# Dealing the gate and up weights' contraction rows four neighbours to a partition

## The chip, the cores and the metric

One core of one Trainium2 chip runs the kernel. The metric is the device time of one execution in microseconds, as the median of several runs. Beside it there is one profiled execution, whose trace gives every duration below.

## The reference

The input is x, 2048 tokens of 512 features in bfloat16 (`A_x`). The tokens are normalized, and two branches work on the result; the input `B_x` is not used.

```python
def reference(A_x, A_w_r, A_w_i, B_x, B_w_gate, B_w_up, B_w_down):
    ...
    x = A_x
    xn = _layernorm(x, axis=-1)
    return x + _A_ref(xn, A_w_r, A_w_i) + _B_ref(xn, B_w_gate, B_w_up, B_w_down)
```

Branch A is a two-dimensional real Fourier transform over tokens and features, a product with complex weights (2048 x 257), and the inverse transform. Branch B is a gated feed-forward layer: gelu(xn Wg) times (xn Wu), then a product with Wd. Wg and Wu are 512 x 1792, Wd is 1792 x 512.

## The kernel before

**Tokens.** Partition p holds tokens 16p to 16p+15, so `x_t` and `xn` are [128, 16 chunks, 512 features]. A chunk c is the 128 tokens 16p+c. Normalization takes mean and variance of a chunk on DVE (`f_stats` line 339, `f_mean` line 342). Chunks 0 to 3 are then normalized on DVE (`f_norm_v`, line 345): chunk 0 in two halves of 256 features (`xn_`, line 386), the others whole. Chunks 4 to 15 are normalized on ACT with a scale and a bias for each token (line 456).

**Transposed tokens.** The feed-forward products contract over features, so they need tokens with features on the partitions: `xnT[b]`, [128, 4 blocks e, 4 chunks, 128 tokens]. Chunks 0 to 3 are transposed by PE, one block of 128 features at a time (`f_T`, line 351, xn as the stationary operand), and copied out of PSUM by DVE or ACT (`f_Tc`, line 354). Chunks 4 to 15 are transposed by DMA (line 459).

**Gate and up weights.** `Wg_sb` and `Wu_sb` are [128, 4, 1792]. Before the change partition i holds the rows i, 128+i, 256+i and 384+i (lines 222 and 223). They are loaded in column slices of 512, 512 and 768, between the loads of x, all on SP's queue (lines 281 to 306); the second slice of Wg comes in two halves of two blocks each. Block e of the weights meets block e of `xnT`, and four matmuls over e give one product of 128 outputs (`mm`, line 494; `mm_part`, line 502).

**Feed-forward units.** A unit is a range of tokens by a range of outputs. PE computes its gate product in PSUM (tag G, two buffers) and its up product (tag U, two buffers); ACT takes gelu (`f_ge`, line 507); DVE multiplies (`f_h`, line 512) into `hT`. The first units are small (one or two chunks), the later ones 512 tokens by 128 outputs. The products with Wd come last (`mm` in `down`, line 829), followed by the last spectral product (line 833), the sum with x (line 836) and the store.

**Spectral branch.** `forward` takes four chunks at a time (groups 0 to 3). The transform over features uses the symmetry of cosines and sines: `fold_a` (line 571) adds and subtracts features d and 511-d into `A`, `fold_b` (line 577) does the same with 256 features and gives `xf`, four kinds q of 128 features each. PE multiplies xf with `RF_t` (bp, line 589), ACT stores the result as `Bs` (line 559), and `group` multiplies that with the matrices F0 to F3 (dp, line 647), whose rows are the 128 folded features. The rest of the branch doesn't see the order of features.

**Order of the work.** The order of instructions on every engine is fixed when the program is built. Each step is added to a `Plan` with an assumed duration, a latency, a key, a release time and the buffers that it takes and gives back; `Plan.order` (line 149) plays them through and writes each engine's instructions in the order in which that play starts them. Its landing times for loads are the constants LAND, WG_LAND and WU_LAND (lines 308 to 311). At run time only semaphores hold an engine up, and each engine works through its list in order.

```python
    WG_LAND = [6.1] * 4 + [10.15] * 4 + [13.2] * 6
    WU_LAND = [7.6] * 4 + [11.7] * 4 + [15.2] * 6
...
        u = split("u_ps", "U", Wu_sb, (1001.4, 1001.5, 1003.1, 1003.5)[k] if k < 4 else 1000.5 + k, WU_LAND, (2, m, 1)[k] if k < 3 else m)
```

At the start PE runs 37 matmuls on zeros, transposes chunk 0, runs 11 more matmuls whose result isn't used (`spin_on`, line 324), and then begins with the gate product of chunk 0.

Of the kernel before, what the change touches and what calls it, by code (L numbers as in the profile page):

```python
# [10 lines left out]
P = 128  # L11
# [17 lines left out]
def _tables():  # L29

    cols, parts, off = {}, [], 0

    def add(name, arr):
        nonlocal off
        arr = np.asarray(arr, dtype=np.float64).reshape(P, -1)
        cols[name] = (off, arr.shape[1])
        parts.append(arr)
        off += arr.shape[1]

    p = np.arange(P)[:, None]
    G, a = np.arange(64) // 4, np.arange(64) % 4
    freq = 16 * a + 8 * (G % 2) + G // 2
    ka = freq[None, :]
    RF = np.zeros((P, NC, 2, 64))
    for c in range(NC):
        th = 2 * np.pi * ((16 * p + c) * ka % S) / S
        RF[:, c, 0] = np.cos(th)  # L50
        RF[:, c, 1] = -np.sin(th)
        RF[:, c, 1, 0] = np.where(p[:, 0] % 2 == 0, 1.0, -1.0)

    d = np.arange(P)[:, None] + 0.5
    j = np.arange(P)[None, :]
    j1 = np.where(j == 0, 128, j)
    FB = [np.cos(2 * np.pi * 2 * j * d / D), np.sin(2 * np.pi * 2 * j1 * d / D),  # L60
          np.cos(2 * np.pi * (2 * j + 1) * d / D), np.sin(2 * np.pi * (2 * j + 1) * d / D)]
    for q in range(4):
        add(f"F{q}", FB[q])

    c = np.arange(NC)[:, None]
    kb = np.arange(NC)[None, :]
    cosk = np.cos(2 * np.pi * c * kb / NC)  # L70
    sink = np.sin(2 * np.pi * c * kb / NC)
    ph = 2 * np.pi * c * (64 + 128 * (kb - 8)) / S
    lo = kb < 8
    alt = np.where(np.arange(P) % 2 == 0, 1.0, -1.0)

    def packed(m0, m, back):
        out = np.zeros((NC, 2, 4, 2, NC, 4))
        for r in range(2):
            for r2 in range(2):
                for a in range(4):  # L80
                    out[:, r, a, r2, :, a] = (m0 if a == 0 else m)[r][r2]
        out = out.reshape(P, P)
        return out.T if back else out

    gen = [[cosk, -sink], [sink, cosk]]
    z_ri = np.where(lo, -sink, 0.0)
    z_ri[:, 0] = np.where(np.arange(NC) % 2 == 0, 1.0, -1.0)
    z = [[np.where(lo, cosk, 0.0), z_ri],
         [np.where(lo, 0.0, np.cos(ph)), np.where(lo, 0.0, -np.sin(ph))]]
    add("L", packed(gen, gen, False))  # L90
    add("L0", packed(z, gen, False))
    for q in range(4):
        add(f"I{q}", FB[q].T)
    add("M", packed(gen, gen, True))
    add("M0", packed(z, gen, True))

    RI = np.zeros((2, 64, NC, P))
    kac = freq[:, None]
    pr = np.arange(P)[None, :]
    sc = 2.0 / (S * D)  # L100
    for cc in range(NC):
        th = 2 * np.pi * ((16 * pr + cc) * kac % S) / S
        RI[0, :, cc] = sc * np.cos(th)
        RI[1, :, cc] = -sc * np.sin(th)
        RI[1, 0, cc] = sc * alt
    def low(a):
        return a.reshape(P, -1).astype(np.float32).astype(ml_dtypes.bfloat16)

    h, kb, a = np.arange(P) // 64, np.arange(P) // 4 % 16, np.arange(P) % 4
    base = 16 * a + 8 * h + 128 * kb
    ks = np.where((h == 0) & (a == 0) & (kb >= 8), 64 + 128 * (kb - 8), base)
    idx = np.zeros((P, 3), dtype=np.int32)
    idx[:, 0] = ks
    idx[:, 1] = (S - ks) % S
    idx[0, 1] = S // 2
    idx[:, 2] = (S - base - 8) // 8
    return low(np.concatenate(parts, axis=1)), cols, low(RF), low(RI), idx
# [82 lines left out]
def kernel(  # L202
# [16 lines left out]

    x_v = A_x.rearrange("b (p c) d -> p c (b d)", c=NC)  # L220
    out_v = out.rearrange("b (p c) d -> p c (b d)", c=NC)
    wg_v = B_w_gate.rearrange("(e i) f -> i e f", e=NE)
    wu_v = B_w_up.rearrange("(e i) f -> i e f", e=NE)
    wd_v = B_w_down.rearrange("(fc f) d -> f fc d", fc=NFC)

    pc = ctx.enter_context(tc.tile_pool(name="pc", bufs=1))
# [121 lines left out]
    def f_T(c, e0, n):  # L348
        tiles["T", c, e0] = tp = ps.tile([P, n, P], BF16, name="tp", tag="S", bufs=4)
        for e in range(n):  # L350
            T_.transpose(tp[:, e], xn[:, c, (e0 + e) * P:(e0 + e + 1) * P], ident)  # L351

    def f_Tc(c, e0, n, copy=V.tensor_copy):
        copy(out=xnT[0][:, e0:e0 + n, c, :], in_=tiles["T", c, e0][:])  # L354
# [19 lines left out]
    def first_two():  # L374
# [5 lines left out]
            o["last"] = o[k]  # L380

        def T(c, h):
            o["T", c, h] = add("PE", 0.12, lambda: f_T(c, 2 * h, 2), [o["xn", c, h]], key=-2000 + 2 * c + h,
                               lat=0.36, acq=("S",))

        def xn_(c, h):
            v(("xn", c, h), lambda: f_norm_v(c, 256 * h, 256), 0.27, [("recip", c)], lat=0.4)

        def stats(c):
            v(("stats", c), lambda: f_stats(c), 0.6, t_min=LAND[c], lat=0.7)  # L390
# [12 lines left out]
        stats(1)  # L403

        recip(0)
        xn_(0, 0)
        mean(1)
        xn_(0, 1)
        T(0, 0)
        T(0, 1)  # L410
        add("PE", 0.61, spin_on, [o["T", 0, 1]], key=-1500, lat=0.61, after=o["T", 0, 1])
# [5 lines left out]
        v("copy1", lambda: f_Tc(0, 2, 2), 0.25, [("T", 0, 1)], lat=0.4)  # L417
        o["copy1"].rel = ("S",)
        xT_op[0] = o["copy1"]
        xn_op[0] = o["xn", 0, 1]  # L420
        v("xn1", lambda: f_norm_v(1, 0, D), 0.33, [("recip", 1)], lat=0.45)
        o["t", 0] = add("PE", 0.12, lambda: f_T(1, 0, 2), [o["xn1"]], key=1000.04, lat=0.3, acq=("S",))
        o["t", 1] = add("PE", 0.12, lambda: f_T(1, 2, 2), [o["xn1"]], key=1000.05, lat=0.3, acq=("S",),
# [27 lines left out]
    def later_four(c0, km, kx):  # L451
        m = [moments(c, km + 0.1 * c) for c in range(c0, c0 + 4)]
        m = [add("POOL", ROOT, lambda: root_eps(c0, 4), m, key=c0, lat=ROOT + 0.1)]
        m = [add("POOL", 0.7, lambda: bias(c0, 4), m, key=c0 + 1, lat=0.9)]
        for c in range(c0, c0 + 4):
            xn_op[c] = add("ACT", 0.72, lambda c=c: A.activation(  # L456
                out=xn[:, c, :], in_=x_t[:, c, :], func=AF.Identity, bias=nb[:, c:c + 1],
                scale=rstd[:, c:c + 1]), m, key=kx + 0.1 * c)
            xT_op[c] = add("SP", 1.3, lambda c=c: nc.sync.dma_start_transpose(
                out=xnT[c // 4][:, :, c % 4, :], in_=xn[:, c, :]), [xn_op[c]], key=c, lat=4.0, t_min=24.0)  # L460
# [102 lines left out]
    def forward(cg, kv):  # L563
        b = {}
        xs = xn[:, 4 * cg:4 * cg + 4, :]
        lo, hi = xs[:, :, 0:256], xs[:, :, 511:255:-1]

        def fold_a(s):
            if s == 0:
                b["A"] = pw.tile([P, 4, 2, 256], BF16, name="A", bufs=1)  # L570
            V.tensor_tensor(out=b["A"][:, :, s, :], in0=lo, in1=hi, op=ALU.subtract if s else ALU.add)  # L571

        def fold_b(s):
            if s == 0:
                b["xf"] = pw.tile([P, 4, 4, P], BF16, name="xf")
            q = slice(2, 0, -1) if s else slice(0, 4, 3)
            V.tensor_tensor(out=b["xf"][:, :, q, :], in0=b["A"][:, :, :, 0:128], in1=b["A"][:, :, :, 255:127:-1],
                            op=ALU.subtract if s else ALU.add)

        src = [xn_op[c] for c in range(4 * cg, 4 * cg + 4)]  # L580
        f = add("DVE", 0.61, lambda: fold_a(0), src, key=kv, acq=("A",), t_min=16.0)
        f = add("DVE", 0.61, lambda: fold_a(1), [f], key=kv + 0.1, lat=0.61)
        f = add("DVE", 0.61, lambda: fold_b(0), [f], key=kv + 0.2, lat=0.61, acq=("xf",))
        f = add("DVE", 0.61, lambda: fold_b(1), [f], key=kv + 0.3, rel=("A",))

        def mm(q):
            b[q] = bp = ps.tile([P, 4, P], F32, name="bp", tag="S", bufs=4)
            for j in range(4):
                T_.matmul(bp[:, j], lhsT=b["xf"][:, j, q, :], rhs=RF_t[:, 4 * cg + j, :], start=True, stop=True)  # L589

        def out(q):
            o = Bs[:, q].rearrange("p g c r a -> p (c r) g a")[:, 8 * cg:8 * cg + 8]
# [300 lines left out]
```

## Time and profile before

| | |
|---|---|
| median of three runs | 178.22 us |
| lowest and highest | 178.19 and 178.55 us |
| the profiled execution | 178.62 us |
| its span, first to last instruction | 176.9 us |
| granted TensorE clock | 1.00 |
| bytes read from and written to HBM | 13.38 and 2.10 MB |

Durations of single operations, from the list of groups by shape (mean ns of one):

| operation | ns |
|---|---|
| xn on DVE, 256 features (line 345) | 330 |
| xn on DVE, 512 features (line 345) | 408 |
| xn on ACT, 512 features (line 456) | 812 |
| fold_a, 1024 elements (line 571) | 676 |
| fold_b, 1024 elements (line 577) | 684 |
| tensor_tensor on 512 bf16 in SBUF (line 684) | 421 |
| hT product, 512 elements, one input in PSUM (line 512) | 688 |
| weight load for a transpose (line 351) | 97 |

A line of a group names the source line, the engine, the operation, the tile written and the tiles read with their shapes, the count, the busy time in us and the mean in ns, and after the last bar the idle time of the engine just before it and what ended that. A line of the timeline begins with the start in us from the span's start and the duration in us. PE is TensorE's matmuls, PEld its weight loads, SPq the DMA instructions on SP.

### The profile page before, as it was taken

The page shows a single profiled execution, that of the slowest core. Times are in us where ns is not written, and L with a number is a line of the kernel's source. Part 1 is how long each engine was busy: PE and PEld are TensorE (multiplying, and loading weights), DVE is VectorE, ACT ScalarE, POOL GpSimd, SP SyncE. Part 2 cuts the span into 40 slices and gives each one's busy share as a digit, 9 for nine tenths or more (in the row PEclk, how much of TensorE's full clock was granted, in tenths as well). Part 3 has the DMA queues.
Part 4 walks back from the last instruction along what each step waited for, and adds up shares of the span by engine and source line. Part 5 has one row for each costly group of instructions (what it writes and reads, how often), then busy time and mean ns, then how long its engine had stood idle before and what let it go on. Part 6 is the DMA issues. An engine that isn't in the chain of part 4 may idle for free.

```text
span 176.9 us, 3143 instructions
## 1 busy us (share of the span) xinstructions
PE 172.8 (98%) x1150; PEld 96.9 (55%) x1150; DVE 115.9 (66%) x255; ACT 96.0 (54%) x171; POOL 17.2 (10%) x38
## 2 busy tenths in 40 slices
PE   7999999999999999999999999999999999999993
PEld 7798845455545554555555455454445445444463
DVE  2588999987434599979899999643516325345333
ACT  3452489799736988898899965362112111211200
POOL 1020340506760000000000000000000000000000
DMA  3999999233717802211201510200122221221212
GB/s 99 323 387 377 371 199 151 60 64 71 246 41 238 299 0 59 59 30 35 59 19 42 152 47 15 59 0 4 59 89 89 77 75 60 89 88 60 82 40 59
DMA packets 21743, 19.35 MB, mean 109 GB/s; under 512 B 8480, under 2 KB 20000, under 8 KB 21728
## 3 DMA queue, kind: packets, MB, share of 16 engines
q1 hardware_dynamic: 21312, 17.84, 36.4%
q0 software_dynamic: 416, 1.32, 2.6%
q8 instruction: 9, 0.15, 0.4%
q14 instruction: 6, 0.05, 0.1%
HBM read 13.38 MB, written 2.10 MB: 87 GB/s over the span
## 4 chain that ended last, share of the span: by engine, by line
PE 95%; DVE 2%; DMA 1%; issue 0%
PE u_ps L494 27%; PE y_ps L829 27%; PE g_ps L494 25%; PE g_ps L502 2%; PE bp L589 2%; PE yp L780 2%; PE gp L750 2%; PE dp L647 2%; PE y_ps L833 2%; PE ep L656 2%; DMA x_t<-in_A_x_dram 1%; DVE stats L339 1%; PE tp L351 1%; DVE xn L345 0%; DVE xnT L354 0%; DVE y_sb L836 0%
## 5 line engine op out<-in xcount | busy, mean ns | idle before, releaser
L494 PE MATMUL u_ps<-xnT,Wu_sb 128*128 128x512 bf16 (+2 forms) x272 | 57.1, 341 | 0.0
L494 PE MATMUL g_ps<-xnT,Wg_sb 128*128 128x512 bf16 (+1 forms) x224 | 53.3, 364 | 0.0
L829 PE MATMUL y_ps<-Wd_sb,hT 128*128 128x512 bf16 (+2 forms) x252 | 51.1, 355 | 0.0
L512 DVE TENSOR_TENSOR hT<-u_ps,ge 128x512 bf16<-128x512 f32 x56 | 38.4, 688 | 18.1 <-PE u_ps L494 16.5
L507 ACT ACTIVATE ge<-g_ps 128x512 bf16<-128x512 f32 x56 | 33.5, 601 | 22.3 <-PE g_ps L494 18.3
L494 PEld LDWEIGHTS <-Wu_sb 128*128 128x128 bf16 x272 | 24.8, 98 | 20.7
L829 PEld LDWEIGHTS <-hT 128*128 128x128 bf16 x252 | 23.2, 98 | 22.4
L494 PEld LDWEIGHTS <-Wg_sb 128*128 128x128 bf16 x224 | 21.5, 98 | 20.5
L786 ACT CAST yf<-yp 128x512 bf16<-128x512 f32 x16 | 9.3, 586 | 40.5 <-PE yp L780 40.5
L836 DVE TENSOR_TENSOR y_sb<-y_ps,y_sb 128x512 bf16<-128x512 f32 (+2 forms) x18 | 11.1, 632 | 30.0 <-PE y_ps L833 30.0
L661 ACT CAST E<-ep 64x512 bf16<-64x512 f32 x32 | 18.5, 579 | 1.4 <-PE ep L656 1.0
L339 DVE BATCH_NORM_STATS2 stats<-x_t 128x6 f32<-128x512 bf16 x16 | 10.4, 674 | 3.9 <-DMA x_t<-in_A_x_dram 3.9
L456 ACT ACTIVATE xn<-x_t,nb,rstd 128x512 bf16<-128x512 bf16 x12 | 9.5, 812 | 1.0 <-POOL nb L370 1.0
L559 ACT CAST ds<-dp 128x512 bf16<-128x512 f32 x16 | 9.2, 597 | 0.8 <-PE dp L647 0.8
L559 ACT CAST Gs<-gp 128x512 bf16<-128x512 f32 x16 | 8.7, 591 | 0.6 <-PE gp L750 0.5
L559 ACT CAST Bs<-bp 128x512 bf16<-128x512 f32 x16 | 8.3, 606 | 0.5 <-PE bp L589 0.5
L792 DVE TENSOR_TENSOR lv<-yf 128x512 bf16<-128x512 bf16 x16 | 6.1, 421 | 1.5 <-ACT yf L786 0.6
L780 PEld LDWEIGHTS <-Gs 128*128 128x128 bf16 x64 | 4.8, 98 | 3.5
L799 DVE TENSOR_TENSOR yt<-lv 128x512 bf16<-128x512 bf16 x16 | 6.1, 421 | 0.3
L833 PE MATMUL y_ps<-yt,RI_t 128*128 128x512 bf16 (+2 forms) x18 | 6.1, 355 | 0.0
L780 PE MATMUL yp<-CT,Gs 128*128 128x128 bf16 x64 | 6.0, 219 | 0.0
L571 DVE TENSOR_TENSOR A<-xn 128x1024 bf16<-128x1024 bf16 x8 | 5.2, 676 | 1.0 <-ACT xn L456 1.0
(65 smaller groups left out, 125.5 us busy)
## 6 DMA issues: line engine op xcount, KB each, us to landing
F<-F SPq DMA_DIRECT2D x32, 64.0 KB, 2.0
y_sb<-in_A_x_dram SPq DMA_DIRECT2D x16, 128.0 KB, 2.1
out_dram<-y_sb SPq DMA_DIRECT2D x15, 128.0 KB, 1.7
Wd_sb<-in_B_w_down_dram SPq DMA_DIRECT2D x1, 1792.0 KB, 7.6
x_t<-in_A_x_dram SPq DMA_DIRECT2D x5, 256.0 KB, 9.8
Wu_sb<-in_B_w_up_dram SPq DMA_DIRECT2D x2, 512.0 KB, 6.2
Wg_sb<-in_B_w_gate_dram SPq DMA_DIRECT2D x1, 768.0 KB, 10.2
Wu_sb<-in_B_w_up_dram SPq DMA_DIRECT2D x1, 768.0 KB
```

The source lines that it names most:

```text
L339: V.bn_stats(out=st[:], in_=x_t[:, c, :])
L456: xn_op[c] = add("ACT", 0.72, lambda c=c: A.activation(out=xn[:, c, :], in_=x_t[:, c, :], func=AF.Identity, bias=nb[:, c:c + 1], scale=rst ...
L494: T_.matmul(b[name][:, f], lhsT=W_[:, e, (f0 + f) * P:(f0 + f + 1) * P], rhs=rhs[:, e, :], start=(e == 0), stop=(e == NE - 1))
L507: A.activation(out=b["ge"][:], in_=b["g_ps"][:], func=AF.Gelu_apprx_tanh)
L512: V.tensor_tensor(out=hT_of(sb, f0, m, o, w), in0=b["u_ps"][:], in1=b["ge"][:], op=ALU.mult)
L559: A.copy(out=o, in_=i)
L661: A.copy(out=b["E"][64 * h:64 * h + 64, r], in_=b["ep", h][64 * r:64 * r + 64])
L780: T_.matmul(t[:, q], lhsT=late["G"][:, q, c0 + j], rhs=IQ[q], start=(q == 0), stop=(q == 3), skip_group_check=True)
L786: A.copy(out=b["yf"][:, j], in_=b[j][:])
L829: T_.matmul(b[o][:], lhsT=hT_of(sb, f, 1, cl * P, P)[:, 0], rhs=Wd_sb[:, f, o:o + w], start=(f == 0), stop=False)
L833: T_.matmul(b[o][:], lhsT=late["RI"][:, c, :], rhs=late["yt"][:, c, o:o + w], start=False, stop=True)
L836: V.tensor_tensor(out=b["y"][:, o:o + w], in0=b[o][:], in1=b["y"][:, o:o + w], op=ALU.add)
```

## The change

The rows of Wg and Wu are dealt differently: partition i now holds the rows 4i to 4i+3, and block e is the row 4i+e of each partition. The tokens must come in the same order of features, so block e of `xnT` is now the features e, 4+e, 8+e and so on:

- For chunks 0 to 3 `xn` stays in its natural order, and the transpose on PE reads every fourth feature. Chunk 0 is normalized in one operation, since each transposed block now needs all 512 features.
- For chunks 4 to 15 ACT reads x with a step of four and writes `xn` permuted (e, i); the DMA transposes are the same as before.
- The folds of groups 1 to 3 work on permuted features: they go through four blocks e with runs of 64 (fold_a) and 32 (fold_b), the mirrored input with blocks and runs reversed. Group 0 has natural order; its fold_a is unchanged, and its fold_b writes with a step of 32 so that `xf` ends in the permuted order.
- `xf` is laid out as [2, 4 chunks, 2, 128] in place of [4 chunks, 4, 128], and the rows of F0 to F3 are permuted to match.
- The planner's numbers change: 0.36 for chunk 0's normalization, and 1.1 in place of 0.61 for group 0's two fold_b steps.

```diff
--- before.py
+++ after.py
@@ -60,7 +60,7 @@
     FB = [np.cos(2 * np.pi * 2 * j * d / D), np.sin(2 * np.pi * 2 * j1 * d / D),
           np.cos(2 * np.pi * (2 * j + 1) * d / D), np.sin(2 * np.pi * (2 * j + 1) * d / D)]
     for q in range(4):
-        add(f"F{q}", FB[q])
+        add(f"F{q}", FB[q].reshape(32, 4, P).transpose(1, 0, 2))
 
 
 
@@ -219,8 +219,8 @@
 
     x_v = A_x.rearrange("b (p c) d -> p c (b d)", c=NC)
     out_v = out.rearrange("b (p c) d -> p c (b d)", c=NC)
-    wg_v = B_w_gate.rearrange("(e i) f -> i e f", e=NE)
-    wu_v = B_w_up.rearrange("(e i) f -> i e f", e=NE)
+    wg_v = B_w_gate.rearrange("(i e) f -> i e f", e=NE)
+    wu_v = B_w_up.rearrange("(i e) f -> i e f", e=NE)
     wd_v = B_w_down.rearrange("(fc f) d -> f fc d", fc=NFC)
 
     pc = ctx.enter_context(tc.tile_pool(name="pc", bufs=1))
@@ -348,7 +348,7 @@
     def f_T(c, e0, n):
         tiles["T", c, e0] = tp = ps.tile([P, n, P], BF16, name="tp", tag="S", bufs=4)
         for e in range(n):
-            T_.transpose(tp[:, e], xn[:, c, (e0 + e) * P:(e0 + e + 1) * P], ident)
+            T_.transpose(tp[:, e], xn[:, c, :].rearrange("p (i e) -> p e i", e=NE)[:, e0 + e], ident)
 
     def f_Tc(c, e0, n, copy=V.tensor_copy):
         copy(out=xnT[0][:, e0:e0 + n, c, :], in_=tiles["T", c, e0][:])
@@ -380,11 +380,11 @@
             o["last"] = o[k]
 
         def T(c, h):
-            o["T", c, h] = add("PE", 0.12, lambda: f_T(c, 2 * h, 2), [o["xn", c, h]], key=-2000 + 2 * c + h,
+            o["T", c, h] = add("PE", 0.12, lambda: f_T(c, 2 * h, 2), [o["xn", c]], key=-2000 + 2 * c + h,
                                lat=0.36, acq=("S",))
 
-        def xn_(c, h):
-            v(("xn", c, h), lambda: f_norm_v(c, 256 * h, 256), 0.27, [("recip", c)], lat=0.4)
+        def xn_(c):
+            v(("xn", c), lambda: f_norm_v(c, 0, D), 0.36, [("recip", c)], lat=0.5)
 
         def stats(c):
             v(("stats", c), lambda: f_stats(c), 0.6, t_min=LAND[c], lat=0.7)
@@ -403,9 +403,8 @@
         stats(1)
 
         recip(0)
-        xn_(0, 0)
+        xn_(0)
         mean(1)
-        xn_(0, 1)
         T(0, 0)
         T(0, 1)
         add("PE", 0.61, spin_on, [o["T", 0, 1]], key=-1500, lat=0.61, after=o["T", 0, 1])
@@ -417,7 +416,7 @@
         v("copy1", lambda: f_Tc(0, 2, 2), 0.25, [("T", 0, 1)], lat=0.4)
         o["copy1"].rel = ("S",)
         xT_op[0] = o["copy1"]
-        xn_op[0] = o["xn", 0, 1]
+        xn_op[0] = o["xn", 0]
         v("xn1", lambda: f_norm_v(1, 0, D), 0.33, [("recip", 1)], lat=0.45)
         o["t", 0] = add("PE", 0.12, lambda: f_T(1, 0, 2), [o["xn1"]], key=1000.04, lat=0.3, acq=("S",))
         o["t", 1] = add("PE", 0.12, lambda: f_T(1, 2, 2), [o["xn1"]], key=1000.05, lat=0.3, acq=("S",),
@@ -454,7 +453,8 @@
         m = [add("POOL", 0.7, lambda: bias(c0, 4), m, key=c0 + 1, lat=0.9)]
         for c in range(c0, c0 + 4):
             xn_op[c] = add("ACT", 0.72, lambda c=c: A.activation(
-                out=xn[:, c, :], in_=x_t[:, c, :], func=AF.Identity, bias=nb[:, c:c + 1],
+                out=xn[:, c, :].rearrange("p (e i) -> p e i", e=NE),
+                in_=x_t[:, c, :].rearrange("p (i e) -> p e i", e=NE), func=AF.Identity, bias=nb[:, c:c + 1],
                 scale=rstd[:, c:c + 1]), m, key=kx + 0.1 * c)
             xT_op[c] = add("SP", 1.3, lambda c=c: nc.sync.dma_start_transpose(
                 out=xnT[c // 4][:, :, c % 4, :], in_=xn[:, c, :]), [xn_op[c]], key=c, lat=4.0, t_min=24.0)
@@ -563,30 +563,45 @@
     def forward(cg, kv):
         b = {}
         xs = xn[:, 4 * cg:4 * cg + 4, :]
-        lo, hi = xs[:, :, 0:256], xs[:, :, 511:255:-1]
+        if cg:
+            xs = xs.rearrange("p c (e i) -> p c e i", e=NE)
+            lo, hi = xs[:, :, :, 0:64], xs[:, :, ::-1, 127:63:-1]
+        else:
+            lo, hi = xs[:, :, 0:256], xs[:, :, 511:255:-1]
 
         def fold_a(s):
             if s == 0:
                 b["A"] = pw.tile([P, 4, 2, 256], BF16, name="A", bufs=1)
-            V.tensor_tensor(out=b["A"][:, :, s, :], in0=lo, in1=hi, op=ALU.subtract if s else ALU.add)
+            o = b["A"][:, :, s, :]
+            V.tensor_tensor(out=o.rearrange("p c (e i) -> p c e i", e=NE) if cg else o, in0=lo, in1=hi,
+                            op=ALU.subtract if s else ALU.add)
 
         def fold_b(s):
             if s == 0:
-                b["xf"] = pw.tile([P, 4, 4, P], BF16, name="xf")
-            q = slice(2, 0, -1) if s else slice(0, 4, 3)
-            V.tensor_tensor(out=b["xf"][:, :, q, :], in0=b["A"][:, :, :, 0:128], in1=b["A"][:, :, :, 255:127:-1],
-                            op=ALU.subtract if s else ALU.add)
+                b["xf"] = pw.tile([P, 2, 4, 2, P], BF16, name="xf")
+            o, a = b["xf"][:, s].rearrange("p c t d -> p (c t) d"), b["A"][:].rearrange("p c t d -> p (c t) d")
+            if cg:
+                o, a = (t.rearrange("p n (e i) -> p n e i", e=NE) for t in (o, a))
+                a = a[:, :, :, 0:32], a[:, :, ::-1, 63:31:-1]
+            else:
+                o = o.rearrange("p n (e i) -> p n i e", e=NE)
+                a = (t.rearrange("p n (i e) -> p n i e", e=NE) for t in (a[:, :, 0:128], a[:, :, 255:127:-1]))
+                a = tuple(a)
+            V.tensor_tensor(out=o, in0=a[0], in1=a[1], op=ALU.subtract if s else ALU.add)
+
+        def xf_of(j, q):
+            return b["xf"][:, int(q in (1, 2)), j, q % 2, :]
 
         src = [xn_op[c] for c in range(4 * cg, 4 * cg + 4)]
         f = add("DVE", 0.61, lambda: fold_a(0), src, key=kv, acq=("A",), t_min=16.0)
         f = add("DVE", 0.61, lambda: fold_a(1), [f], key=kv + 0.1, lat=0.61)
-        f = add("DVE", 0.61, lambda: fold_b(0), [f], key=kv + 0.2, lat=0.61, acq=("xf",))
-        f = add("DVE", 0.61, lambda: fold_b(1), [f], key=kv + 0.3, rel=("A",))
+        f = add("DVE", 0.61 if cg else 1.1, lambda: fold_b(0), [f], key=kv + 0.2, lat=0.61, acq=("xf",))
+        f = add("DVE", 0.61 if cg else 1.1, lambda: fold_b(1), [f], key=kv + 0.3, rel=("A",))
 
         def mm(q):
             b[q] = bp = ps.tile([P, 4, P], F32, name="bp", tag="S", bufs=4)
             for j in range(4):
-                T_.matmul(bp[:, j], lhsT=b["xf"][:, j, q, :], rhs=RF_t[:, 4 * cg + j, :], start=True, stop=True)
+                T_.matmul(bp[:, j], lhsT=xf_of(j, q), rhs=RF_t[:, 4 * cg + j, :], start=True, stop=True)
 
         def out(q):
             o = Bs[:, q].rearrange("p g c r a -> p (c r) g a")[:, 8 * cg:8 * cg + 8]
```

## The prediction

> **What bounds the kernel now.** I read the page first: the busy row and the chain that ended last.
>
> ```profile
> PE 172.8 (98%) x1150; PEld 96.9 (55%) x1150; DVE 115.9 (66%) x255; ACT 96.0 (54%) x171; POOL 17.2 (10%) x38
> ...
> PE 95%; DVE 2%; DMA 1%; issue 0%
> ```
>
> TensorE is busy 98% of the span and carries 95% of the chain. The page warns that a busy PE can hide gaps, so I asked next what PE ever waits for. The list of waits has these entries for PE and its weight loads, beside the first matmul of all:
>
> ```profile
> PEld L351 <- DVE xn L345: 0.7, 2, 0.5
> ...
> PE tp L351 <- DVE xn L345: 0.2, 1, 0.2
> PEld L502 <- DMA Wg_sb<-in_B_w_gate_dram: 0.2, 1, 0.2
> ```
>
> All of them lie before 6.7 us. From there to 174.2 us I compared start to start in the trace: the 128-column matmuls follow each other by 56 ns, the 256-column ones by 109 ns, and the only hole over 12 ns is 0.07 us at 12.39, between the transposes of chunks 2 and 3. So nothing on DVE, ACT or the queues costs time unless it makes PE wait, and a gain can come only from starting PE's stream earlier. Third view, the timeline of the start (start, duration, engine, line):
>
> ```profile
> 5.01 0.34 DVE L345 TENSOR_SCALAR xn<-x_t,mv,rstd 128x256 bf16<-128x256 bf16 x1
> 5.28 0.17 DVE L342 BATCH_NORM_AGGREGATE mv<-stats 128x2 f32<-128x6 f32 x1
> 5.37 0.31 DVE L345 TENSOR_SCALAR xn<-x_t,mv,rstd 128x256 bf16<-128x256 bf16 x1
> ...
> 5.74 0.29 DVE L354 COPY xnT<-tp 128x256 bf16<-128x256 bf16 x1
> ...
> 6.06 0.29 DVE L354 COPY xnT<-tp 128x256 bf16<-128x256 bf16 x1
> 6.27 0.40 DVE L345 TENSOR_SCALAR xn<-x_t,mv,rstd 128x512 bf16<-128x512 bf16 x1
> ...
> 6.66 0.23 PEld L502 LDWEIGHTS <-Wg_sb 128*128 128x128 bf16 x4 [0.20 <-DMA Wg_sb<-in_B_w_gate_dram]
> ...
> 6.84 0.27 PEld L351 LDWEIGHTS <-xn 128*128 128x128 bf16 x4
> ```
>
> Two things meet here. The first gate matmuls start at 6.66, when the first piece of Wg has landed. After four of them PE transposes chunk 1, whose normalization ends at 6.27+0.40 = 6.67; a transpose begins about 0.06 us after its xn (5.35 to 5.41 for chunk 0), so it is ready at 6.73 and goes at 6.84: 0.11 us to spare. Fourth view, PE's weight loads around 12 us, and the landing of the second piece of Wu, asked of its tile:
>
> ```profile
> 10.42 1.68 PEld L502 LDWEIGHTS <-Wg_sb 128*128 128x128 bf16 x16
> 12.19 0.55 PEld L351 LDWEIGHTS <-xn 128*128 128x128 bf16 x8
> 12.69 0.59 PEld L494 LDWEIGHTS <-Wu_sb 128*128 128x128 bf16 x6
> ```
>
> ```profile
> L277 SPq DMA_DIRECT2D Wu_sb<-in_B_w_up_dram x1: 468/468/468, 4.9 to 4.9; - x1
> ...
> DMA to landing us min/median/max: 7.1/7.1/7.1
> ```
>
> Issued at 4.89, this piece lands at 4.89+7.1 = 12.0. Its first use is at 12.69, so today it is 0.7 us early.
>
> **What the skill says.** "VectorE: DVE Perf Modes", section on mode 2x_1P: two bf16 results per cycle need step +1 or -1 in every tensor. The trace agrees: line 577, reversed input included, does 1024 bf16 in 684 ns, which is what line 512 needs for 512 elements read from fp32 (688). "SBUF — State Buffer", specifications: lines are 16 bytes and an access pattern needs two hits per line for full rate. A step of four bf16 has two hits, a step of 32 has one. The trace shows no step above two in a read of SBUF. "TensorE: Matmul & The Clock Gate", section on weight-path perf modes: the fast weight load takes any column step up to 1,024. The trace agrees for a step of two: F is read so at line 750, at 98 ns like everything else. "DMA: Bandwidth & Descriptors", section on the semaphore's 16: one descriptor moves one contiguous run of the last dimension.
>
> ```profile
> L456 ACT ACTIVATE xn<-x_t,nb,rstd 128x512 bf16<-128x512 bf16 x12 | 9.5, 812 | 1.0 <-POOL nb L370 1.0
> L577 DVE TENSOR_TENSOR xf<-A 128x1024 bf16<-128x1024 bf16 x8 | 5.3, 684 | 0.0
> L750 PEld LDWEIGHTS <-F 128*128 128x128 bf16 x64 | 4.3, 98 | 2.1
> ```
>
> **Part by part.**
>
> *Weight loads (lines 222, 223).* The loads stay column slices, so a run is still 1,024 or 1,536 bytes and the number of packets is the same. The trace has the 1,024-byte packets at 46 ns each in the median, which with 16 engines is 356 GB/s, and row order isn't in that figure. Slow ones stand at the start of a transfer (up to 0.55 us each), and neighbouring rows may make them fewer or more. Value taken: 0; bound from both sides: 5% of the time to landing, that is 0.35 us either way for the second piece of Wu. A gain is nearly worthless: with Wg at once, PE still waits for chunk 1's transpose.
>
> *Chunk 0 normalized in one operation.* Two of 0.34 and 0.31 become one of about 0.41 (the 512-wide row, 408 ns in the list by shape). It ends at 5.42 in place of 5.35, so the first copy moves from 5.74 to 5.81 and ends at 6.10: before 6.66, cover Wg's landing. The mean, the second reciprocal, copy 1 and chunk 1's xn follow 0.07 later, and xn ends at 6.74, transpose ready at 6.80, needed at 6.84. Cost 0; without that 0.04 us it would be up to 0.07. If Wg landed earlier the transpose would be the wait, and the gain ends at 0.04.
>
> *Transposes with step 4 (line 351).* 16 weight loads. Value: 98 ns as now, cost 0, since step two is free. Upper bound: each takes twice as long, 12 of them inside the packed stream, 12 x 0.1 = 1.2 us. No gain is possible, the matmul sets the 56 ns.
>
> *The planner's order.* The orders of instructions on each engine show one move that touches PE's data: half of unit 2's up product (4 matmuls on the second piece of Wu) now stands before the transposes of chunks 2 and 3, after 12 instead of 16 gate matmuls. PE is there at 10.42 + 12 x 0.109 = 11.73, the weights at 12.0: **a new wait of 0.27 us**, and behind it in PE's queue stand both transposes and everything else. The hole of 0.07 at 12.39 goes, because xn of chunk 3 (ends 12.46) is then early. Net +0.20. The planner's own due time for these weights, 11.7 in WU_LAND, is earlier than the landing, so it doesn't see the wait.
>
> *Folds.* In groups 1 to 3 the innermost runs shrink to 64 and 32 but keep step 1 or -1: 0.68 us each as now, cost 0. In group 0 line 577's two writes get step 32 and lose the packed mode: the slope of the bf16 rows (421 ns at 512, 684 at 1024) is 263 ns for 256 cycles, so 1024 cycles are 1055 ns over the fixed 158: 1.21 us, +0.53 each, on DVE. Cover: in the trace the second fold ends at 28.29 and its matmul (bp, line 589) starts at 29.41. The new order drops the stats between the folds and puts bp one up product (0.86) later, at 30.27. The second fold ends at 25.81+1.13+0.61+1.21 = 28.76 (operations overlap by 0.08). Spare 1.4 us; the hT product queued between them ends at 27.6 and its PSUM is wanted after 29.4. Cost 0. Both ends: 0.68 (mode kept), 2.27 (two cycles per element).
>
> *ACT's normalization with step-4 reads, 12 times.* Two hits per line: 0.81 us as now, cost 0. Upper bound 0.43 more each if the read runs at half rate. A gain has no source. The matrices F0 to F3 are permuted when the program is built; the DMA transposes read xn as before.
>
> **Sum.** 0 + 0 + 0 + 0.20 + 0 + 0 = +0.20 us. The profiled execution took 178.62 us for a span of 176.92; the median of the runs is 178.22, and the difference is put on that: **178.42 us**. What this kernel's measurement can tell from no change is about 0.2%, 0.36 us, so the forecast is "no difference".
>
> **Rivals.**
> - *The weights come early enough* (20%). The new row order lands Wu 0.27 us or more sooner; the wait and the old hole both go: 178.15 us. For: the slow first packets. Against: the 46 ns don't depend on rows.
> - *The weights come later* (17%, slower). At 5% the wait at 11.73 becomes 0.27+0.35, net +0.55 plus up to 0.3 at the first Wg: 178.8 to 179.1. It decides from 0.16 us of lateness.
> - *The strided fold writes hold up bp* (10%, slower). Place: group 0, line 577, then PE at 30.27. At two cycles per element the second fold ends at 25.81+2.19+0.61+2.27 = 30.88, PE waits 0.67 with its handover: 178.42+0.67 = 179.1. It decides once a fold takes more than about 1.95 us. For: one hit per line. Against: only writes are strided, and ACT's writes in 8-byte pieces (Bs, 606 ns) cost nothing over dense ones (yf, 586).
> - *Step-4 reads are slow* (7%, slower). Transposes +1.2 us, or ACT late with ge in its fullest stretch (21 to 47 us), four times 0.43 = 1.7 before POOL's waits take it up: 179.6 to 180.1.
> - *An earlier start that I don't see* (4%, faster): 177.8.
> The forecast itself keeps 42%. Faster by over 0.2%: 4%; within: 42+20 = 62%; slower: 17+10+7 = 34%. Range: 178.0 to 179.3; beyond it lie the slow reads and the early start, about 11% together.
>
> **What would show it.** Right: PE's only wait after 7 us is a weight load of L494 for Wu's landing, 0.2 to 0.3 us near 11.8; group 0's folds at 1.2 us, all others at 0.68; xn on ACT at 0.81; LDWEIGHTS of xn at 98 ns. Wrong: a PE wait for xf near 30 us (folds), ge rows waiting for ACT (reads), 1,024-byte packets off 46 ns or Wg's first use off 6.66 by more than 0.1 (loads).

## The result and the profile after

The changed kernel takes 187.09 us (median of 4 runs, 186.83 to 187.62) where the kernel before takes 178.38 beside it (178.19 to 178.71): 1.049 times the time, interval 1.046 to 1.0519. The forecast was 178.42 with a range up to 179.3. The profiled execution took 186.83 us for a span of 185.1, so the span grew by 8.2 us.

The page of the changed kernel, the same parts as before: busy time, the slices of TensorE and of its clock, the chain that ended last, and the row of the second folds (line 590, formerly 577).

```profile
PE 175.0 (95%) x1132; PEld 98.7 (53%) x1150; DVE 123.4 (67%) x254; ACT 96.7 (52%) x171; POOL 20.9 (11%) x38
...
PE   7999996299999999999999999999999999999993
...
PEclk9999999759999999999999999999999999999999
...
PE 87%; DMA 4%; DVE 3%; SPq 2%; issue 2%; DVEq 0%
...
L590 DVE TENSOR_TENSOR xf<-A 128x1024 bf16<-128x1024 bf16 x8 | 13.2, 1674 | 0.1
```

Read the slices first: each is 4.6 us wide, TensorE drops to 6 and 2 in the seventh and eighth (about 28 to 37 us) and nowhere else; the clock row has a 7 and a 5 in the eighth and ninth. The last row names a suspect: eight operations with a mean of 1674 ns, where they had 684. A mean can hide two kinds, so the next view is the tile's own, with minimum, median and maximum:

```profile
L590 DVE TENSOR_TENSOR xf<-A x8: 682/688/4642, 26.3 to 51.0; 128x1024 bf16<-128x1024 bf16 x8
```

Most take 0.68 us; the longest takes 4.64. The timeline of VectorE (start, duration, engine, line) shows which:

```profile
26.31 4.63 DVE L590 TENSOR_TENSOR xf<-A 128x1024 bf16<-128x1024 bf16 x1
30.57 0.90 DVE L512 TENSOR_TENSOR hT<-u_ps,ge 128x512 bf16<-128x512 f32 x1
31.38 4.64 DVE L590 TENSOR_TENSOR xf<-A 128x1024 bf16<-128x1024 bf16 x1
```

They are the two folds of group 0 whose writes go at a step of 32 elements: 4.6 us for 1024 elements, 4.5 ns each, where the forecast had 1.21 us and an upper bound of 2.27. TensorE's timeline shows what that does:

```profile
31.51 1.02 PE L494 MATMUL u_ps<-xnT,Wu_sb 128*128 128x512 bf16 x4 [1.60 <-DVE hT L512]
...
36.08 1.46 PE L604 MATMUL bp<-RF_t,xf 128*128 128x128 bf16 x12 [3.32 <-DVE xf L590]
...
39.04 1.91 PE L494 MATMUL u_ps<-xnT,Wu_sb 128*128 128x512 bf16 x4
40.75 1.21 PE L494 MATMUL g_ps<-xnT,Wg_sb 128*128 128x512 bf16 x4
```

Three losses stand in these lines. The product hT was queued behind the first fold, so its PSUM came free late (1.60 us). The second fold itself was late (3.32 us). And the four up matmuls at 39.04 occupy 1.91 us where those at 31.51 occupied 1.02: TensorE is running slowly. The granted clock by stretches (the last three figures of a line: clock, DMA share, GB/s):

```profile
33.00:36.00 3.00, 0.00 (x0) 0.00 (x0) 3.00 (x2) 2.39 (x4) 0.00 (x0) 0.71 0.57 115
36.00:39.00 3.00, 2.70 (x15) 1.86 (x17) 3.00 (x9) 1.07 (x2) 0.00 (x0) 0.50 0.28 57
39.00:43.00 4.00, 4.00 (x15) 1.64 (x14) 3.07 (x8) 2.08 (x4) 2.52 (x4) 0.74 0.00 0
```

Cut finer, the same view has nothing but 1.00 and 0.50 beside two stretches in which the clock changes, so the means tell when: 0.71 from 33 to 36 us puts the fall at about 34.3, and 0.74 from 39 to 43 the return at about 41.1. From 36.08 to 40.75 TensorE started 12 matmuls of 128 columns and 8 of 512; at the 56 and 216 ns of the full clock that is 2.4 us, and it took 4.67: 2.3 us lost. "TensorE: Matmul & The Clock Gate", the section on what is actually happening, describes such a clock: after an idle window of about 3.4 us it is halved, and it returns after about as long of sustained work. This trace agrees on the half, but not on the times. The clock fell only 1.5 us into the wait for xf; before that lay 1.6 us of waiting for hT and 1.25 us of work. It came back 5.0 us after work had begun again. The wait of 1.6 us alone left it at 1.00 (e2, below).

Start to start against the kernel before, TensorE lost 0.1 at the first gate matmul, 0.3 for Wu's second piece, 1.8 behind hT, 3.5 behind xf and 2.4 to the clock: 8.1 of the 8.2 us.

### The profile page after: what moved, and what is told of

The parts are those of the page before. It is cut to its first block, busy times and chain, and to the rows that moved or that the text cites. A ratio compares the mean times of both kernels' runs of the same rounds, so it can differ in the third digit from the quotient of the medians.

```text
span 185.1 us, 3124 instructions
## 1 busy us (share of the span) xinstructions
PE 175.0 (95%) x1132; PEld 98.7 (53%) x1150; DVE 123.4 (67%) x254; ACT 96.7 (52%) x171; POOL 20.9 (11%) x38
## 4 chain that ended last, share of the span: by engine, by line
PE 87%; DMA 4%; DVE 3%; SPq 2%; issue 2%; DVEq 0%
PE y_ps L844 26%; PE u_ps L494 25%; PE g_ps L494 24%; DMA Wu_sb<-in_B_w_up_dram 4%; DVE xf L590 2%; PE bp L604 2%; PE yp L795 2%; PE gp L765 2%; PE dp L662 2%; PE y_ps L848 2%; PE ep L671 2%; SPq L277 1%; SPq L273 1%; DVE hT L512 0%; PE tp L351 0%
## 5 line engine op out<-in xcount | busy, mean ns | idle before, releaser
L494 PE MATMUL u_ps<-xnT,Wu_sb 128*128 128x512 bf16 (+2 forms) x266 | 57.9, 344 | 2.1 <-DVE hT L512 1.6
L590 DVE TENSOR_TENSOR xf<-A 128x1024 bf16<-128x1024 bf16 x8 | 13.2, 1674 | 0.1
L604 PE MATMUL bp<-RF_t,xf 128*128 128x128 bf16 x64 | 5.0, 236 | 3.3 <-DVE xf L590 3.3
L604 PEld LDWEIGHTS <-xf 128*128 128x128 bf16 x64 | 4.4, 107 | 4.4 <-DVE xf L590 3.5
```

What stands on the lines that cost most here:

```text
L494: T_.matmul(b[name][:, f], lhsT=W_[:, e, (f0 + f) * P:(f0 + f + 1) * P], rhs=rhs[:, e, :], start=(e == 0), stop=(e == NE - 1))
L590: V.tensor_tensor(out=o, in0=a[0], in1=a[1], op=ALU.subtract if s else ALU.add)
L604: T_.matmul(bp[:, j], lhsT=xf_of(j, q), rhs=RF_t[:, 4 * cg + j, :], start=True, stop=True)
```

## The experiments

The kernel before ran at a median of 178.5 us beside e1 to e4, 178.47 beside e5 to e7 and 178.62 beside e8 to e10.

| run | what it is | median us | ratio to before, interval |
|---|---|---|---|
| e1 | group 0's second folds read with step 4, write densely | 180.25 | 1.0111 (1.0085 to 1.0137) |
| e2 | only the first of the two writes with step 32 | 183.53 | 1.0304 (1.0273 to 1.0336) |
| e3 | changed kernel, TensorE kept busy while it waits for xf | 186.39 | 1.0429 (1.0409 to 1.0450) |
| e4 | kernel before, only the rows of the weights dealt | 178.72 | 1.0016 (1.0008 to 1.0024) |
| e5 | e1 in the old order | 179.86 | 1.0083 (1.0065 to 1.0102) |
| e6 | kernel before in the new order | 178.60 | 1.0005 (0.9997 to 1.0014) |
| e7 | e1, ScalarE reads densely | 179.24 | 1.0048 (1.0031 to 1.0065) |
| e8 | changed kernel, group 0's folds as before | 179.13 | 1.0029 (1.0017 to 1.0041) |
| e9 | e8 in the old order | 179.01 | 1.0022 (1.0012 to 1.0031) |
| e10 | the dealing done by VectorE's normalization | 179.20 | 1.0041 (1.0023 to 1.0058) |

**Is it the write step?** My theory after the result: the step of the write, and nothing else in the new folds, makes them long. Rivals: the late start of the folds, or the clock alone.

e1, the step moved from the write to the reads:

```diff
-                o = o.rearrange("p n (e i) -> p n i e", e=NE)
-                a = (t.rearrange("p n (i e) -> p n i e", e=NE) for t in (a[:, :, 0:128], a[:, :, 255:127:-1]))
-                a = tuple(a)
+                o = o.rearrange("p n (e i) -> p n e i", e=NE)
+                a = tuple(t.rearrange("p n (i e) -> p n e i", e=NE) for t in (a[:, :, 0:128], a[:, :, 255:127:-1]))
```

> The changed kernel, with group 0's two second folds turned round: they read A with a step of four and write xf densely; everything else and the order of the work as in the changed kernel. Theory W (the write step of 32 costs about four cycles per element, 4.63 us per fold in the profile after): each fold falls to about 1.2 us (one element per cycle), both PE waits near 30 us and the half clock after them go, and what is left is the later first use of Wg (0.17) and the wait for Wu (0.29): 178.4 + 0.5 = 178.8 us. Rival R (any step other than one in a bf16 operand costs that much, read or written): folds stay near 4.6 us, 187 us. Rival L (the loads or ACT's strided reads carry part of the loss): well over 179.5 us with short folds.

Measured 180.25. The view of its tile xf:

```profile
L589 DVE TENSOR_TENSOR xf<-A x8: 679/688/1215, 26.4 to 44.6; 128x1024 bf16<-128x1024 bf16 x8
```

The same sums on the same data now take 1.22 us, TensorE no longer waits for xf, and its clock stays full. So 6.8 of the 8.7 us hang on the write's step. But the time is 1.4 us above what I expected, and in that part rival L holds: something else carries loss too. That opened a second question, taken up below.

e2, the first fold as in the changed kernel and the second as in e1 (a branch `elif s:` with e1's lines stands before `else:`):

> The changed kernel, with only the second of group 0's two second folds turned round (step-four reads, dense write); the first keeps its step-32 write. Theory: the hT product queued behind the first fold still makes PE wait 1.9 us for its PSUM buffer, the wait for xf (3.5 us) goes, and a PE pause of 1.9 us alone doesn't bring the clock down: 178.4 + 0.5 + 1.9 = 180.8 us, granted clock 1.00 after 30 us. Rival (any pause near 2 us brings the half clock too): 182.5 us or more. Rival (the loss is linear in the folds' time): half of 8.7 us, 182.7 us.

Measured 183.53, 2.7 us above what I expected. One such fold costs 3.3 us over e1, the other 3.6 more. TensorE lost 1.6 us behind hT as in the changed kernel; of waits for xf only 0.2 was left, and the clock was full. Much of the rest, which I had not expected, went near 44 to 46 us, where TensorE waits for a later group's xf (the 0.2) and for ScalarE (0.6).

e3, to take the clock's part by itself:

```diff
+            if cg == 0 and q == 1:
+                for k in range(58):
+                    T_.matmul(bp[:, 0], lhsT=spin[:], rhs=spin[:], start=True, stop=True)
```

> The changed kernel with 58 matmuls on zeros, 56 ns each, put between group 0's first and second set of bp matmuls, so that PE computes through the 3.5 us in which it waits for xf. Theory C (the pause brings TensorE's clock to half for about 5 us afterwards, and that is 2.4 us of the loss): clock stays at 1.00 and the time falls to 187.1 - 2.4 = 184.7 us. Rival (PE runs slowly after the pause because of its inputs, SBUF or PSUM traffic): time unchanged at 187 us, and matmuls after 36 us still 0.43 us apart.

Measured 186.39: the half clock is gone (clock 1.00 over the span), but only 0.7 us came back. In its profile TensorE now lost 1.9 us, start to start, between 47 and 58 us, where the changed kernel loses nothing: it waits 0.2 us for a later group's xf and, for ScalarE, 0.6 at bp and 0.6 at g_ps. (Through later weights this execution, the slowest of its four, was already 0.6 us behind the changed kernel's at 13 us.) So the clock's 2.4 us aren't an independent loss here. My reading, which no run separates, is that ScalarE caught up while TensorE ran at half speed.

e4, the rest of the change's loads alone (lines 222 and 223 of the kernel before with the new row order; the products then pair features with other rows):

> The kernel before with nothing but the rows of Wg and Wu dealt as four neighbours per partition; the tokens keep their order, so the products pair the wrong features. It shows what the loads alone do. Theory: each weight load takes SP 0.1 to 0.2 us longer to issue (0.69, 0.62, 0.56, 0.55 and 0.65 us in the profile after against 0.43, 0.51, 0.47, 0.43 before), the transfers themselves run at the same rate, the first use of Wg moves by 0.1 us and nothing else waits: 178.5 us. Rival (the longer issue comes from the rest of the change): issue times as before, 178.4 us. Rival (neighbouring rows transfer faster): first use of Wg below 6.6 us.

Measured 178.72, 0.2 to 0.3 us over before. SyncE's timeline of the changed kernel shows a likely source:

```profile
2.19 0.69 SPq L277 DMA_DIRECT2D Wg_sb<-in_B_w_gate_dram  x1
...
5.32 0.56 SPq L277 DMA_DIRECT2D Wu_sb<-in_B_w_up_dram  x1
```

Before, these two issues took 0.43 and 0.47 us, and the second piece of Wu was issued at 4.89, so here it leaves 0.43 us later. Its transfer isn't slower (7.0 us to landing against 7.1). e4 issues at the same pace (0.69 and 0.56 us), but that this makes up its 0.2 to 0.3 us is not shown: its profiled execution, 179.81 us, was its slowest, with 7.9 us to landing.

**Why is the dense write still 1.7 us over before?** e1's list of waits has these for ScalarE and TensorE:

```profile
ACT xn L455 <- POOL nb L370: 2.4, 2, 1.5
...
PE g_ps L494 <- ACT ge L507: 0.6, 1, 0.6
...
PE bp L603 <- ACT Bs L559: 0.2, 1, 0.2
```

ScalarE is late around 42 to 51 us: start to start TensorE loses 0.4 us at 43.1 and 0.7 at 51.0. Two theories: the planner's new order (ORDER), or the longer operations (OPERATIONS: twelve normalizations at 0.85 in place of 0.81 us, two folds at 1.22).

e5, in e1:

```diff
-    WU_LAND = [7.6] * 4 + [11.7] * 4 + [15.2] * 6
+    WU_LAND = [7.6] * 4 + [12.3] * 4 + [15.2] * 6
-        f = add("DVE", 0.61 if cg else 1.1, lambda: fold_b(0), [f], key=kv + 0.2, lat=0.61, acq=("xf",))
-        f = add("DVE", 0.61 if cg else 1.1, lambda: fold_b(1), [f], key=kv + 0.3, rel=("A",))
+        f = add("DVE", 0.61, lambda: fold_b(0), [f], key=kv + 0.2, lat=0.61, acq=("xf",))
+        f = add("DVE", 0.61, lambda: fold_b(1), [f], key=kv + 0.3, rel=("A",))
```

> The dense-write kernel (folds of group 0 read A with step 4 and write xf dense), with the planner's numbers changed: its fold_b estimate for group 0 back from 1.1 to 0.61, and the landing of the second up piece at 12.3 instead of 11.7. Up to 45 us TensorE's work then stands in the order of the kernel before. Theory ORDER: the 0.8 to 1.1 us that TensorE lost to late ScalarE work between 42 and 52 us came from the new order, so this runs at 178.7 to 179.0 (178.5, and 0.25 for the loads). Theory OPERATIONS: it came from the longer operations themselves (12 step-4 normalizations at 0.03 us more each, two folds of 1.22), so it stays at 179.7 to 180.2.

e6, the reverse of the last four lines, in the kernel before:

> The kernel before with one change: the planner's estimate for the two fold_b of group 0 is 1.1 instead of 0.61 us, so that TensorE and ScalarE get the order of the changed kernel around the folds; no operation differs. Theory ORDER: waits on ScalarE appear between 42 and 52 us, 179.2 to 179.6. Theory OPERATIONS: 178.5 as before.

179.86 and 178.60: ORDER falls twice. The new order of the folds costs nothing, and the old one brings back 0.4 us of 1.7, part of which is Wu's wait. e5 has the order of the kernel before around the folds, so the two can be laid side by side. ScalarE's normalization of two of the next chunks in the kernel before:

```profile
35.08 1.52 ACT L456 ACTIVATE xn<-x_t,nb,rstd 128x512 bf16<-128x512 bf16 x2 [0.68 <-POOL nb L370]
```

and e5:

```profile
36.37 1.61 ACT L455 ACTIVATE xn<-x_t,nb,rstd 128x512 bf16<-128x512 bf16 x2 [1.74 <-POOL nb L370]
```

GpSimd's bias for these chunks comes 1.3 us later (it starts at 36.10 instead of 34.80): behind the two folds on VectorE (0.54 us longer each) stand the statistics that GpSimd waits for. ScalarE sits idle for 1.74 us, does its normalizations afterwards, and near 41 us TensorE loses 1.1 us at bp, to ScalarE's evacuations and to a later group's xf.

e7, in e1, ScalarE's part alone:

```diff
-                out=xn[:, c, :].rearrange("p (e i) -> p e i", e=NE),
-                in_=x_t[:, c, :].rearrange("p (i e) -> p e i", e=NE), func=AF.Identity, bias=nb[:, c:c + 1],
+                out=xn[:, c, :], in_=x_t[:, c, :], func=AF.Identity, bias=nb[:, c:c + 1],
```

> The dense-write kernel with ScalarE's normalization of chunks 4 to 15 reading x in its own order instead of with step 4 (these chunks' features then meet the wrong rows of the weights). The normalization goes back from 0.84 to about 0.81 us. Theory ORDER: no change beside the dense-write kernel, 180.0 to 180.3. Theory OPERATIONS: about half of the late time goes, 179.5 to 179.8.

Measured 179.24, below what either theory said: 12 x 0.05 us of ScalarE's time give back 1.0 us (here and below, of the excess over the kernel before beside each). So the two causes aren't a sum; ScalarE has a little room, and past it TensorE waits. That made the theory CHAIN, against READS.

e8, group 0's folds as in the kernel before (`a = a[:, :, 0:128], a[:, :, 255:127:-1]`, dense write), all else as changed:

> The changed kernel with group 0's folds left as they were before: dense reads, dense write, natural order (so that group 0's folded features meet rows of the tables in another order). All else of the change stays: loads, transposes with step 4, chunk 0 in one operation, ScalarE's step-4 reads, the planner's numbers. Theory CHAIN (ScalarE is late because VectorE's longer folds delay the statistics of the next chunks, these GpSimd's bias, this the normalization, and the step-4 reads add to it; either half taken away leaves enough room): 178.9 to 179.3, being 178.5 and the loads and the wait for the second up piece. Theory READS (the step-4 reads alone make ScalarE late): 179.9 to 180.3, as the dense-write kernel.

e9, e8 with the planner's numbers of e5:

> The kernel of the run before this one with the planner's numbers of the kernel before (0.61 for every fold) and the second up piece's landing at 12.3. Theory CHAIN: 178.7 to 178.9, what the loads alone cost. Theory READS: 179.5 to 179.9, as the dense-write kernel in the old order.

179.13 and 179.01, in CHAIN's range and 0.1 above it, far from READS. In e8 the list of waits has none of TensorE for ScalarE between 13 and 60 us. The folds' 0.54 us twice therefore cost 1.2 us in one order (e1 less e8) and 1.0 in the other (e5 less e9), though nothing waits for group 0's xf. Step-4 reads on ScalarE cost 1.0 with the long folds (e1 less e7) and at most 0.3 without (e8 less e4, which also holds Wu's wait).

How the folds' length reaches ScalarE is shown less well than that it does. In e9's profile, with short folds in e5's order, the bias still starts at 35.66, and TensorE still loses 0.7 us at bp near 41; so most of e5's 1.3 us above can't be put on the folds. Between e1 and e8 there is a second way, beside the statistics. GpSimd's multiplication for the chunks before is stretched, in e1:

```profile
26.91 0.78 POOL L369 TENSOR_TENSOR nb<-mv,rstd 128x4 f32<-128x4 f32 x1
```

and in e8:

```profile
27.01 0.30 POOL L369 TENSOR_TENSOR nb<-mv,rstd 128x4 f32<-128x4 f32 x1
```

In both it ends with VectorE's first fold (27.64 in e1, 27.26 in e8). ScalarE then waits for this bias 0.85 us in e1 and 0.32 in e8, and over the run 2.4 us against 1.4. So in the order of e1 and e8 long folds make ScalarE late by way of GpSimd, as CHAIN has it. How much goes through the statistics and how much through GpSimd being held was not taken apart.

e10, the permutation at another place, with e5's numbers; transposes and all folds are then dense (their lines are left out here):

```diff
-        V.tensor_scalar(out=xn[:, c, o:o + w], in0=x_t[:, c, o:o + w], scalar1=mv[:, c, 0:1],
+        V.tensor_scalar(out=xn[:, c, :].rearrange("p (e i) -> p e i", e=NE),
+                        in0=x_t[:, c, :].rearrange("p (i e) -> p e i", e=NE), scalar1=mv[:, c, 0:1],
```

> The change in another place: VectorE's normalization of chunks 0 to 3 reads x with step 4 and writes the dealt order densely, so that the transposes and all folds are dense; planner's numbers as in the run before. The normalization should take about 0.65 instead of 0.41 us (step-4 reads at one element a cycle, as the step-4 folds). Theory CHAIN: 178.9 to 179.5: 178.8 and up to 0.25 for chunk 0, which is on the way to the first matmul, and up to 0.4 at chunks 2 and 3. Theory READS: above 179.8.

Measured 179.20, within its range. The normalization takes 544 ns in place of 410 (0.65 us was expected), and TensorE waits 0.2 us for chunk 1 and 0.6 for chunks 2 and 3. This is the best form of the whole change that ran: 7.9 us faster than the changed kernel and still slower than the kernel before.

**What a write step costs.** m1 measures VectorE and ScalarE by themselves, each operation on 1024 bf16 elements a partition.

> Writes zeros only; it measures operations of 128x1024 bf16 elements by themselves, three times each: VectorE tensor_tensor with its write at steps 1, 2, 4, 8, 16, 32 and 64, in the changed kernel's own nesting, in runs of 2, 4, 8 and 16 neighbours at a step of 64 bytes, with its reads at steps 4 and 32, and in fp32 at 64 and 128 bytes; copies on VectorE and ScalarE with such writes and reads. Theory STEP: the write costs by its distance in bytes, so up to step 8 it is about 1.2 us (the plain one-a-cycle rate), rises after that and reaches 4.6 us at 64 bytes; reads at any step stay at 1.2 us. Theory NARROW: any write that isn't to neighbours costs the 4 cycles, so step 2 already takes 4.6 us. In either, runs of 2 and 4 neighbours divide the cost by 2 and 4. With fp32 at 64 bytes: 4.6 us if distance counts, about 1.2 us if the two-byte write is what costs.

Its list of groups by shape, the rows that matter. Line 49 is dense; 51, 53, 55 and 61 write at steps 2, 4, 8 and 64 (16 and 32, left out, take 4436 and 4605 ns); 63 is the changed kernel's pattern; 65 and 67 write pairs and fours of neighbours at a distance of 64 bytes; 73 and 75 read at steps 4 and 32; 91 is ScalarE's copy with a write at step 32.

```profile
L61 DVE TENSOR_TENSOR o<-a,b 128x1024 bf16<-128x1024 bf16 x3 | 14.1, 4712 | 0.1
L55 DVE TENSOR_TENSOR o<-a,b 128x1024 bf16<-128x1024 bf16 x3 | 14.1, 4692 | 0.1
L91 ACT COPY oa<-a 128x1024 bf16<-128x1024 bf16 x3 | 14.0, 4680 | 0.1
...
L63 DVE TENSOR_TENSOR o<-a,b 128x1024 bf16<-128x1024 bf16 x3 | 13.8, 4586 | 0.1
...
L53 DVE TENSOR_TENSOR o<-a,b 128x1024 bf16<-128x1024 bf16 x3 | 7.3, 2449 | 0.0
...
L75 DVE TENSOR_TENSOR o<-a,b 128x1024 bf16<-128x1024 bf16 x3 | 5.6, 1870 | 0.1
...
L51 DVE TENSOR_TENSOR o<-a,b 128x1024 bf16<-128x1024 bf16 x3 | 3.9, 1303 | 0.0
L73 DVE TENSOR_TENSOR o<-a,b 128x1024 bf16<-128x1024 bf16 x3 | 3.7, 1226 | 0.1
...
L65 DVE TENSOR_TENSOR o<-a,b 128x1024 bf16<-128x1024 bf16 x3 | 3.1, 1021 | 0.1
L67 DVE TENSOR_TENSOR o<-a,b 128x1024 bf16<-128x1024 bf16 x3 | 2.1, 693 | 0.1
...
L49 DVE TENSOR_TENSOR o<-a,b 128x1024 bf16<-128x1024 bf16 x3 | 2.1, 688 | 0.0
```

Both theories were too simple. The cost about doubles from step 2 to 4 and from 4 to 8 and then stands still, so it isn't the distance as such, and step 2 isn't yet the full price. Count the visits of 16-byte lines in the order of writing: a step of 2 puts four elements into each line before it moves on (256 visits), a step of 4 two (512), a step of 8 or more one (1024). Then 2.45 and 4.4 to 4.7 us are 4.8 and 4.3 to 4.6 ns a visit. (Step 2's 1.30 us would be 5.1, but it also lies within 0.1 us of line 73's 1.23, so it doesn't speak for the count.) Pairs of neighbours, 512 visits, take 1.02 us, 2.0 ns a visit; fp32 at 64 bytes takes 1.86 us for 1024 visits, 1.8 ns each; reads at step 32 as well. So in these sums two-byte writes pay about 4.5 ns for each line that they visit, and four-byte ones less than half of it. The changed kernel's pattern, alone on the chip, has its 4.6 us: nothing else in the kernel is needed to explain it. Line 73 reads as e1's fold does: a read with two hits in each line takes 1.23 us, the plain rate, as "SBUF — State Buffer", specifications, has it; for a write two hits (line 53) are not enough.

m2 tests the two-byte reading, and whether such operations hold GpSimd, whose nb multiplication (line 369) took 3.76 us in the changed kernel instead of 0.30:

> Writes zeros only. GpSimd runs a row of 120 multiplications of 128x4 fp32 beside VectorE's operations of 128x1024 bf16: dense tensor_tensor, dense copy, tensor_tensor with reads at step 4, with the write at step 32. If GpSimd is held by VectorE's two-input operations, its operations stretch to 0.7, 1.2 and 4.6 us there and stay at 0.3 us beside copies; if not, 0.3 us throughout. Then VectorE alone: copies with writes at steps 32, 8, 4 and reads at step 4, tensor_scalar with reads at step 4 and the write at step 32, and tensor_tensor with a dense write that starts one element off, and with pairs that start one element off. If the cost is one of two-byte writes that fill no aligned four bytes (4.6 ns for each visit of a 16-byte line), the pairs that start one element off take 2.3 us and more instead of 1.0, the dense write off by one stays at 0.7 to 1.3.

Pairs that start one element off take 2.90 us in place of 1.02, and a dense write one element off stays at 0.70, as expected if whole four-byte words are what is cheap. GpSimd's multiplications beside VectorE, from four stretches of the timeline (beside a dense sum, a sum with step-4 reads, one with the step-32 write, a copy with a step-32 write), and one with VectorE idle:

```profile
7.08 0.65 POOL L52 TENSOR_TENSOR r<-p,q 128x4 f32<-128x4 f32 x1
...
9.91 1.18 POOL L52 TENSOR_TENSOR r<-p,q 128x4 f32<-128x4 f32 x1
...
15.08 4.08 POOL L52 TENSOR_TENSOR r<-p,q 128x4 f32<-128x4 f32 x1
...
30.37 2.33 POOL L52 TENSOR_TENSOR r<-p,q 128x4 f32<-128x4 f32 x1
...
79.97 0.20 POOL L52 TENSOR_TENSOR r<-p,q 128x4 f32<-128x4 f32 x1
```

Each lasts nearly as long as VectorE's operation beside it, so a slow fold is also a slow bias. The description of the kernel says that only semaphores hold an engine up; here none stands between the two, and GpSimd is held. I had expected copies to leave GpSimd alone; they hold it too (2.33 of 2.39 us).

## Why the prediction was wrong

*What bounds the kernel* was read rightly: TensorE's stream has no holes, and the loss is TensorE's waits and its clock, to within 0.1 us. *Transposes with step 4* cost nothing, as said: eight weight loads occupy 0.56 us, before 0.55. *Chunk 0 in one operation* took 410 ns as said, and the first gate matmul waited for Wg, not for it (0.21 us); x had landed 0.46 us earlier in this execution, so its small spare wasn't put to the test. *The planner's order* brought Wu's wait at the place named, 0.51 us in the list of waits (0.39 start to start) where 0.27 was said, because that piece was issued 0.43 us later; e6 shows that the order of the folds itself is free.

*Weight loads* at nothing, with 0.35 us either way: e4 has 0.2 to 0.3. The bound held, but its reason was the wrong one. I looked at packets, which didn't change (46 ns in the median), and not at SyncE's issuing time, which rose by 0.09 to 0.26 us for four of the five loads of whole slices (the last one's fell, from 1.08 to 0.65); it explains the larger wait for Wu. The first gate matmul at 6.77 instead of 6.66 it doesn't explain: with the old loads that matmul starts at 6.17 in e6, with the new ones at 6.55 in e2.

*Folds* is the step that failed, by its size. "1024 cycles are 1055 ns over the fixed 158: 1.21 us" assumes that losing the packed mode is all that a write step costs; "2.27 (two cycles per element)" was no bound: the only two-byte writes at a step in the profile before are copies of four elements (lines 689 and 714, 178 ns each), too few to show a rate. (Their reads go at a step above two as well, which "no step above two in a read of SBUF" overlooks.) Measured: 4.63. The row I set against it, ScalarE's Bs writes in 8-byte pieces, was no evidence: fours of neighbours write at the dense rate (m1, line 67). The rival "the strided fold writes hold up bp" had the mechanism and the point from which it decides, about 1.95 us. With 4.63 in its own sum the second fold ends at 25.81+4.55+0.61+4.63 = 35.6, measured 36.0, and TensorE waits 5.3 us, measured 1.8+3.5; the 1.8 came at hT, ahead of the place it named. What it lacked besides is that such waits can halve the clock.

The cover was wrong too, apart from the size. e1's folds took 1.22 us, the forecast's own figure, and "cost 0" was still off by 1.0 to 1.2 us (e5 less e9, e1 less e8). I followed the folds to bp and hT, and not to what else they delay: the statistics behind them on VectorE, GpSimd's bias, then ScalarE's normalization.

*ScalarE's step-4 reads* at nothing: 0.844 us instead of 0.812. In the changed kernel no wait of TensorE comes from it; e7 shows that it isn't free where ScalarE is already late.

What stays open: why two-byte writes pay by the line, and why a VectorE copy with a step-32 write takes 2.39 us, half of the sum's 4.61. How the 0.3 us between e4 and e8 divides between Wu's wait and ScalarE's reads was not taken apart; e9, planned for Wu's later landing, is only 0.1 us below e8, within the noise. m1 and m2 are one execution each, with three of every operation.

## What to carry to other kernels

Price a permuted write from a row that writes elements of that size in that pattern, and if there is none, measure it or put the step on the read side, or keep neighbours together: a sum of the fold's size takes 4.6 us with 2-byte writes at 64 bytes, 1.2 with step-4 reads, and 0.7 with runs of four. When an operation grows, follow everything that is queued behind it on its engine, and through the engines that this feeds, before calling it covered. And look at the clock after a long wait of TensorE: here it fell to half, though with the clock held at full speed only 0.7 us came back.

## What the runs showed of the hardware

- A bf16 write at a step in VectorE's sums: about 4.5 ns for each 16-byte line visited, at steps 4 to 64; 4.4 to 4.7 us for 1024 elements from a step of 16 bytes on, no more at 128 bytes. ScalarE's copy with a write at step 32 takes the same 4.68 us.
- VectorE's copies and scalar operations with a write at step 32 take half of that, 2.39 us.
- Issuing a load of a whole column slice of the weights took SyncE 0.69, 0.62, 0.56 and 0.55 us with neighbouring rows in one partition, and 0.43, 0.51, 0.47 and 0.43 before (a fifth went the other way, 0.65 against 1.08).
- While VectorE runs a sum or a copy on SBUF, GpSimd's small multiplication of 0.20 us lasts nearly as long as it (0.65, 1.18, 4.08 and 2.33 us above). Beside a memset of 3.47 us it kept its 0.20.
- TensorE's clock fell to 0.50 within a wait, 1.5 us after its start, when 3.1 of the 4.4 us before had been waiting; it was back at 1.00 after 6.8 us, 5.0 of them work. A wait of 1.6 us alone did not lower it.
